# A block of 128 tokens in plain float32 products instead of split ones, with the steps around it in a new order

## The chip, the core and the metric

One NeuronCore of a Trainium2 chip runs the whole program. The metric is the device time of one execution in microseconds, lower is better. The engines are PE (TensorE, matmuls; PEld are its weight loads), DVE (VectorE), ACT (ScalarE), POOL (GpSimd) and SP (SyncE, which issues most DMAs).

## The reference

Three layers in a row on two sequences of 768 tokens (S) with 512 features (D):

```python
# 1. attention in 8 heads, each query only sees keys of its own cluster
scores = np.where(q_assign[..., :, None] == k_assign[..., None, :], scale * q @ k.T, -1e9)
x = softmax(scores) @ v
# 2. gate by a causal convolution over 5 tokens
gate = sigmoid(sum(conv_w[k] * shifted(x, k) for k in range(5)))
x = (gate * (x @ w_val)) @ w_out
# 3. one of 8 experts for each token; a token may keep the expert of the token before it
fresh = argmax(x[s] @ w_gate)
e = fresh if s == 0 or sigmoid(x[s] @ w_local) < 0.5 else prev
out[s] = softmax(x[s] @ w_gate)[e] * (relu(x[s] @ w1[e]) @ w2[e])
```

The choice of the expert hangs on small differences, so products that lead to it are made to float32 accuracy.

## The kernel before, in words

**Stages.** `Attn` (to about 286 us) goes through 8 pairs of heads. `Moe.rest` (286 to 396 us) finishes the last head pair and runs layer 2 for the second sequence, the router (`Route`) and the first block of tokens of layer 3. `Ffn.run` (from 396 us) takes the eight experts one after another, the one with the most tokens first.

**Splits.** A product to float32 accuracy is made of the engine's faster type F32R: each operand is split into a rounded part (`hi`, ACT copies it) and the remainder (`lo`, a subtraction). For the weights, `Ffn.split` (L1344) does this for a slice of 128 x 1024 numbers; eight slices make one expert: slices 0 to 3 are w1 (512 x 256 each), slices 4 to 7 are w2 (256 x 512 each).

**The block that goes ahead.** When the first sequence is routed, `Route.first` (L1089) picks 128 tokens of its most used expert. This is the block with r = -1. It is gathered (`gather`, tile xg-1), turned by PE (`turn`, tile pt-1, L1310), put through w1 (`up`, tiles ph-1, L1383 and L1386) and w2 (`down`, tile po-1, L1422) while the second sequence is still being routed. Its eight slices are ws0 to ws7; their remainders wl0 to wl7 are made on POOL in pieces of 256 columns, those of all later slices (from ws8) on DVE in one piece (L1352 to L1354). Slice buffers `ws` are eight in all (`Ffn.NS`): ws8 takes the place of ws0, and so on.

**The router.** For each half of a sequence (384 tokens, named 00, 01, 10, 11) the chain goes back and forth between PE and DVE: logits (lg, L872, PE), the code of each token's choice (L879 to L966, DVE), a row of codes (row, L972, PE), a running maximum over the tokens (cm, L977, DVE), back to columns (pb, L986, PE), one-hot choices (r_oh, L991 to L994, DVE), the count of equal choices ahead of a token (pp, L1008, PE), the position (r_pos, L1010 to L1014, DVE). `Route.placed` (L1045) makes from it the operands rhs and onr of a product (L1077: plf, plm and pll, PE) that writes the lists of tokens. After half 11, `Route.last` (L1136) ranks the experts into `tbl` (L1157), which SP reads before it can load any slice from ws8 on, and writes the lists `L`; then POOL gathers the tokens of expert 0 (xg0, L1296), PE turns them (pt0), and ACT and DVE write them as x0 (L1313, L1314). The first product with x0 and wh8 (L1378) begins the experts.

**What sets the order.** Each engine runs its instructions in the order in which the program issues them. In the attention that order comes from tables of places (`PLAN`, `LATE`, `MORE`, `FIRST`, `LAG`, `ORDER`, `GO`, and `BESIDE` for layer 2 of the first sequence); in `Moe.rest` from the table `STEPS`, a list of (name, count): each entry advances the named step so many times. `Y` is the product with w_out (tile yp, L858), `V` that with w_val (va, L825), `W` turns rows for the store to `ydr` (yr, L887), `conv` the convolution of the second sequence on DVE (L796), `split` one call of `Ffn.split`.

Of the kernel before, what the change touches and what calls it, by code (L numbers as in the profile page):

```python
# [20 lines left out]
DM = 512  # L21
# [26 lines left out]
class Attn:  # L48
# [1220 lines left out]
class Ffn:  # L1269
# [31 lines left out]
    def turn(self, ps, tag, pool, r, i, width=None):  # L1301

        nc, n = self.nc, self.cap(r)
        if i == 0:
            self.x[r] = pool.tile([128, KD, width or 2 * max(CAPS)], F32R, tag="x", name=f"x{r}")
        x, c0 = self.x[r], 128 * i
        m = min(128, n - c0)
        pt = ps.tile([128, 512], F32, tag=tag, name=f"pt{r}_{i}").rearrange("p (k t) -> p k t", k=KD)
        for k in range(KD):
            nc.tensor.transpose(pt[:, k, :m], self.xg[r][i][:m, 128 * k:128 * k + 128],  # L1310
                                self.rt.ident[:m, :m])
        hv = x[:, :, c0:c0 + m]
        nc.scalar.activation(hv, pt[:, :, :m], AF.Copy)  # L1313
        nc.vector.tensor_tensor(x[:, :, n + c0:n + c0 + m], pt[:, :, :m], f32(hv), op=ALU.subtract)  # L1314
# [29 lines left out]
    def split(self, pool, s, eng=None):  # L1344
# [10 lines left out]
        self.sp[s] = hi, lo  # L1355


    def up(self, ps, pool, r, c):
# [4 lines left out]
        if c == 0:  # L1363
            self.h[r] = [pool.tile([128, KF, 128 if r < 0 else max(CAPS)], F32R, tag=t, name=f"{t}{r}", bufs=1)
                         for t in ("hh", "hl")]
        hh, hl = (t[:, 2 * c:2 * c + 2, :n] for t in self.h[r])
        one = r < 0
        ps = ps.tile([128, 512 if one else 1024], F32, tag="h", name=f"ph{r}_{c}").rearrange(
            "p (m n) -> p m n", m=2)
        for m in range(2):  # L1370
# [3 lines left out]
            for k in range(KD):  # L1374
# [184 lines left out]
class Moe:  # L1559
# [75 lines left out]
    def rest(self, end, close, close_x):  # L1635
# [244 lines left out]
```

## Time and profile before

| | us |
|---|---|
| median of 3 runs | 582.47 |
| the three runs | 583.67, 578.79, 582.47 |
| the profiled execution, its own time | 579.11 |
| its span, first to last instruction | 577.3 |
| around the span | 1.81 |

All durations below are from the profiled execution. Its time lies 3.36 us under the median of the three. Times in rows are counted from the start of the span. An engine's row in a timeline gives the start, the duration, the line and operation, the tile written and the tiles read, how many neighbours are merged (x4), and in brackets how long the engine sat idle before and who released it.

### The profile page before, as it was taken

How to read it: one execution, taken by the hardware profiler on the slowest of the kernel's cores; microseconds unless marked ns; L12 is line 12 of the kernel's file. 1: busy time of each engine (PE TensorE's matmuls, PEld its weight loads, DVE VectorE, ACT ScalarE, POOL GpSimd, SP SyncE). 2: the span in 40 equal slices, each digit the busy share in tenths (PEclk: the TensorE clock that was granted, in tenths of full speed). 3: DMA queues.
4: the chain of work that ended last, by engine and by line, in shares of the span. 5: the costliest groups of instructions: out<-in, count | busy, mean ns of one | idle time of the engine just before them, and what ended most of it. 6: DMA issues, size and time to landing. Idle time of an engine off the chain costs nothing. (4 is left out here: it accounts for less than half of the span.)

```text
span 577.3 us, 9419 instructions
## 1 busy us (share of the span) xinstructions
PE 526.6 (91%) x3336; PEld 392.0 (68%) x3336; DVE 404.9 (70%) x703; ACT 303.2 (53%) x581; POOL 284.0 (49%) x227
## 2 busy tenths in 40 slices
PE   3798989999999999999988999699999999999993
PEld 0564545565555565567577898588989889879892
DVE  3756777888788779757967665886637486587681
ACT  2635454555545566576553244345635467468571
POOL 4475639795979698568920116735003043022011
PEclk9998899999999999899998999799999999999997
DMA  8996283857575625000000047058773877646940
GB/s 192 212 218 188 90 228 103 238 124 201 161 194 131 166 70 138 1 11 1 0 10 0 12 143 267 19 194 272 256 241 119 280 234 231 212 151 215 320 164 13
DMA packets 53180, 86.90 MB, mean 151 GB/s; under 512 B 6313, under 2 KB 30321, under 8 KB 53132
## 3 DMA queue, kind: packets, MB, share of 16 engines
q1 hardware_dynamic: 49996, 78.36, 46.8%
q0 software_dynamic: 3136, 7.92, 4.4%
q8 instruction: 27, 0.44, 0.3%
q14 instruction: 21, 0.17, 0.1%
HBM read 59.65 MB, written 8.62 MB: 118 GB/s over the span
## 5 line engine op out<-in xcount | busy, mean ns | idle before, releaser
L307 DVE TENSOR_REDUCE mn<-mx 128x1 f32<-128x512 f32 (+1 forms) x156 | 94.2, 638 | 31.9 <-PE mx L303 31.8
L398 ACT ACTIVATE p<-s 128x384 f32<-128x384 f32 x168 | 75.7, 486 | 59.5 <-PE s L397 57.6
L476 POOL TENSOR_TENSOR acc<-acc,p 128x768 f32<-128x768 f32 x42 | 85.4, 2054 | 4.2 <-ACT p L398 2.4
L1354 DVE TENSOR_TENSOR wl<-ws,wh 128x1024 fp32r<-128x1024 f32 x64 | 77.4, 1221 | 10.4 <-ACT wh L1349 9.3
L1349 ACT ACTIVATE wh<-ws 128x1024 fp32r<-128x1024 f32 x72 | 74.8, 1056 | 2.4 <-DMA ws<-in_w_dram 2.4
L396 PE MATMUL s<-xq,xk 128*128 128x384 f32 x168 | 64.0, 381 | 6.0 <-ACT p L398 6.0
L1455 POOL DMA_INDIRECT out_dram<-o,L x12 | 13.8, 1153 | 110.8 <-ACT o L1454 93.8
L492 PE MATMUL pv<-p,v 128*64 128x384 f32 x336 | 65.3, 511 | 0.0
L303 PE MATMUL mx<-km,q 80*128 80x512 f32 (+1 forms) x192 | 61.2, 388 | 3.1 <-DVE mn L307 2.8
L396 PEld LDWEIGHTS s<-xq,xk 128*128 128x128 f32 x168 | 31.8, 189 | 38.4 <-issue 22.0
L796 DVE SCALAR_TENSOR_TENSOR gp<-xT,cwt,gp 128x767 f32<-128x767 f32 (+3 forms) x32 | 52.8, 1665 | 6.7 <-ACT gp L790 6.3
L397 PE MATMUL s<-q,km 97*128 97x384 f32 x168 | 57.5, 342 | 0.0
L1383 PE MATMUL ph<-x,wh 128*128 128x384 f32 (+4 forms) x192 | 56.4, 338 | 0.0
L1386 PE MATMUL ph<-x,wl 128*128 128x256 f32 x192 | 51.6, 279 | 0.0
L303 PEld LDWEIGHTS mx<-km,q 80*128 80x128 f32 x192 | 37.4, 207 | 16.1 <-DVE mn L307 8.9
L1422 PE MATMUL po<-wh,hh 128*128 128x512 f32 x96 | 39.0, 406 | 0.0
L492 PEld LDWEIGHTS pv<-p,v 128*64 128x64 f32 x336 | 20.9, 140 | 26.5 <-issue 25.7
L1383 PEld LDWEIGHTS ph<-x,wh 128*128 128x128 f32 x192 | 36.1, 188 | 3.2 <-issue 1.0
L476 POOL TENSOR_TENSOR acc<-p,p 128x768 f32<-128x768 f32 x14 | 26.8, 1928 | 22.4 <-ACT p L398 22.4
L1422 PE MATMUL po<-wh,hl 128*128 128x512 f32 x96 | 37.8, 393 | 0.0
L1422 PE MATMUL po<-wl,hh 128*128 128x512 f32 x96 | 37.6, 391 | 0.0
L1386 PEld LDWEIGHTS ph<-x,wl 128*128 128x128 f32 x192 | 36.0, 188 | 0.1
(376 smaller groups left out, 1162.4 us busy)
## 6 DMA issues: line engine op xcount, KB each, us to landing
ws<-in_w_dram SPq DMA_DIRECT2D x72, 512.0 KB
qt<-in_qT_dram SPq DMA_DIRECT2D x8, 384.0 KB
kt<-in_kT_dram SPq DMA_DIRECT2D x8, 384.0 KB
q<-hiq SPq DMA_DIRECT2D x16, 192.0 KB
km<-hik SPq DMA_DIRECT2D x16, 192.0 KB
v<-in_v_dram SPq DMA_DIRECT2D x8, 384.0 KB
xk<-kt SPq DMA_DIRECT2D x16, 192.0 KB
xk<-hik SPq DMA_DIRECT2D x16, 192.0 KB
```

Source lines behind the costliest of these rows:

```text
L303: nc.tensor.matmul(ps[:, n * p:n * p + n], lhsT=q2[0:80, h, t * 128:t * 128 + 128], rhs=km[0:80, h, c:c + n], start=(p == 0), stop=True, s ...
L307: nc.vector.tensor_reduce(out=out, in_=src, axis=AX.X, op=ALU.max)
L396: nc.tensor.matmul(ps, lhsT=kl[:, h, ks], rhs=t1[:, h, hs], start=True, stop=False)
L397: nc.tensor.matmul(ps, lhsT=km[:97, h, ks], rhs=q2[:97, h, hs], start=False, stop=True)
L398: nc.scalar.activation(pt[:, h, hs], ps, AF.Exp, scale=1.0 / D ** 0.5)
L476: eng.tensor_tensor(t[:, h], p(0)[:, h] if first is None else t[:, h], p(j)[:, h], op=ALU.add)
L492: nc.tensor.matmul(self.pvt[64 * h:64 * h + 64, i, :HS], lhsT=v[:, j, 64 * h:64 * h + 64], rhs=pt[:, h, half(i)], start=False, stop=(j == ...
L1349: nc.scalar.activation(hi, t, AF.Copy)
L1354: (eng or nc.vector).tensor_tensor(lo[:, cs], t[:, cs], f32(hi[:, cs]), op=ALU.subtract)
L1383: nc.tensor.matmul(ps[:, m, :2 * n], lhsT=hi[:, k, ms], rhs=x[:, k, :2 * n], start=st and not (one and m), stop=False, skip_group_check=True)
L1386: nc.tensor.matmul(ps[:, m, :256], lhsT=lo[:, k, ms], rhs=x[:, k, :256], start=False, stop=sp, skip_group_check=True)
L1422: nc.tensor.matmul(self.po[r][i][:m], lhsT=a[:, k, ts], rhs=w[:, q], start=(k == 0 and z == 0), stop=(k == KF - 1 and z == 2))
```

## The change

The block r = -1 loses its splits. `Ffn.turn` makes x-1 as one float32 tile of 128 columns (no remainder on DVE). `Ffn.up_ahead` multiplies the slices ws0 to ws3 as they were loaded with x-1, 128 columns at a time, and one ACT Relu writes the hidden values. `Ffn.down_ahead` multiplies the hidden values with ws4 to ws7 in one pass. So the eight calls of `split` for ws0 to ws7 go: eight ACT copies (L1349) and 32 POOL subtractions (L1354), and with them four ACT copies and eight DVE operations on hidden values (L1391, L1392, L1402). The buffers ws0 to ws7 are now read by PE and free when it has read them. The experts' own path (`up`, `down`) stays as it is. The tables are written anew; a line of one of them stands in the diff.

```diff
-    LAG = (7, 10, 14, 12, 28, 6, 12, 12)
+    LAG = (7, 10, 14, 12, 28, 6, 13, 13)
...
-    def turn(self, ps, tag, pool, r, i, width=None):
+    def turn(self, ps, tag, pool, r, i):
...
-            self.x[r] = pool.tile([128, KD, width or 2 * max(CAPS)], F32R, tag="x", name=f"x{r}")
+            self.x[r] = pool.tile([128, KD, 2 * max(CAPS) if r >= 0 else n],
+                                  F32R if r >= 0 else F32, tag="x", name=f"x{r}")
...
         nc.scalar.activation(hv, pt[:, :, :m], AF.Copy)
+        if r < 0:
+            return
         nc.vector.tensor_tensor(x[:, :, n + c0:n + c0 + m], pt[:, :, :m], f32(hv), op=ALU.subtract)
...
-        n = 1024 if eng is None or eng is nc.vector else 256
-        for c in range(0, 1024, n):
-            cs = slice(c, c + n)
-            (eng or nc.vector).tensor_tensor(lo[:, cs], t[:, cs], f32(hi[:, cs]), op=ALU.subtract)
+        nc.vector.tensor_tensor(lo, t, f32(hi), op=ALU.subtract)
...
+    def up_ahead(self, ps, pool, c):
+        nc, x = self.nc, self.x[-1]
+        w = self.st[c].rearrange("p (k f) -> p k f", k=KD)
...
+        for m in range(2):
+            if m:
+                yield
+            for k in range(KD):
+                nc.tensor.matmul(ps[:, m], lhsT=w[:, k, 128 * m:128 * m + 128], rhs=x[:, k],
+                                 start=(k == m == 0), stop=(k == KD - 1), skip_group_check=True)
+        self.late[c] = lambda: nc.scalar.activation(self.h[-1][:, 2 * c:2 * c + 2], ps[:, 0:2],
+                                                    AF.Relu)
+
+    def down_ahead(self, ps, c):
+        nc = self.nc
+        w = self.st[4 + c].rearrange("p (k f) -> p k f", k=2)
...
+        for q in range(2):
+            k = 2 * c + q
+            nc.tensor.matmul(self.po[-1][0], lhsT=self.h[-1][:, k], rhs=w[:, q], start=(k == 0),
+                             stop=(k == KF - 1))
...
-        split = lambda i: self.f.split(self.wp, i, nc.gpsimd if i < 8 else nc.vector)
+        split = lambda i: self.f.split(self.wp, i)
...
-            "split": each(*((split, i) for i in range(11))),
+            "split": each(*((split, i) for i in range(8, 11))),
```

What the change moves, on three engines. First PE, from the logits of half 11 to the first products of the block, before (an F32R product of 256 columns each, four pairs of which make one half of a slice):

```order
L872 MATMUL lg11_3873<-yT11_3691,wg_416 32x96 x16
L1077 MATMUL plm_3903<-rhsm_3833,onrm_3826 128x48 x3
L1310 MATMUL pt-1_0_3909<-ident_63,xg-1_0_3655 128x128 x4
L887 MATMUL yr101_3922<-ident_63,yT10_3600 128x128 x4
L887 MATMUL yr102_3930<-ident_63,yT10_3600 128x128 x4
L972 MATMUL row11_3945<-ident_63,r_code_2954 1x4x32 x3
L1383 MATMUL ph-1_0_3953<-x-1_3908,wh0_3657 128x256
L1386 MATMUL ph-1_0_3953<-x-1_3908,wl0_3658 128x256
```

and now (lines are those of the changed kernel; L1368 is the product of `up_ahead`):

```order
L887 MATMUL yr101_3824<-ident_63,yT10_3536 128x128 x4
L872 MATMUL lg11_3832<-yT11_3670,wg_416 32x96 x16
L1312 MATMUL pt-1_0_3850<-ident_63,xg-1_0_3665 128x128 x4
L1077 MATMUL plm_3869<-rhsm_3801,onrm_3794 128x48 x3
L972 MATMUL row11_3874<-ident_63,r_code_2954 1x4x32 x3
L1368 MATMUL ph-1_0_3881<-x-1_3849,ws0_3596 128x128 x4
L887 MATMUL yr102_3892<-ident_63,yT10_3536 128x128 x4
L986 MATMUL pb11_3900<-rconst_2942,cm11_3878 32x1 x12
```

One of the row turns now stands ahead of lg11 and one behind row11, the turn of the block ahead of plm, and four float32 products of 128 columns stand where eight F32R products of 256 columns stood.

Second POOL, between the gather of the block and those of expert 0, before (the subtractions of ws0 to ws7):

```order
L1296 DMA xg-1_0_3655<-ydr_62,LA_2962 128x512
L1354 TENSOR_TENSOR wl0_3658<-ws0_3571,wh0_3657 128x256 x4
L1354 TENSOR_TENSOR wl1_3665<-ws1_3573,wh1_3664 128x256 x4
L1354 TENSOR_TENSOR wl2_3672<-ws2_3575,wh2_3671 128x256 x4
L1354 TENSOR_TENSOR wl3_3730<-ws3_3577,wh3_3729 128x256 x4
L1354 TENSOR_TENSOR wl4_3757<-ws4_3579,wh4_3756 128x256 x4
L1354 TENSOR_TENSOR wl5_3818<-ws5_3581,wh5_3817 128x256 x4
L1354 TENSOR_TENSOR wl6_3859<-ws6_3583,wh6_3858 128x256 x4
L1354 TENSOR_TENSOR wl7_3939<-ws7_3585,wh7_3938 128x256 x4
L1296 DMA xg0_0_4131<-ydr_62,L_2963 128x512
```

and now:

```order
L1296 DMA xg-1_0_3665<-ydr_62,LA_2962 128x512
L1296 DMA xg0_0_4042<-ydr_62,L_2963 128x512
L1296 DMA xg0_1_4044<-ydr_62,L_2963 128x512
L1296 DMA xg0_2_4046<-ydr_62,L_2963 64x512
L1296 DMA xg1_0_4135<-ydr_62,L_2963 128x512
```

POOL has no arithmetic left between the gathers.

Third DVE, at the end of the stage, from the remainder of ws8 on (x0 are the tokens of expert 0, LR lists for the stores, L1323 a copy in `tbl` that SP reads ahead of the load of ws11), before:

```order
L1354 TENSOR_TENSOR wl8_4152<-ws8_4071,wh8_4151 128x1024
L1402 SCALAR_TENSOR_TENSOR hl-1_3952<-hs-1_2_4128,hh-1_3951 128x256
L1392 TENSOR_TENSOR hs-1_3_4174<-ph-1_3_4157,hs-1_3_4174 128x2x128
L1402 SCALAR_TENSOR_TENSOR hl-1_3952<-hs-1_3_4174,hh-1_3951 128x256
L1184 TENSOR_SCALAR LR32_2964<-plr_4192,rconst_2942 128x24
L1186 COPY LR32_2964<-plr_4192 128x24
L1184 TENSOR_SCALAR LR64_2965<-plr_4192,rconst_2942 128x24
L1186 COPY LR64_2965<-plr_4192 128x24
L1314 TENSOR_TENSOR x0_4203<-pt0_0_4204,x0_4203 128x4x128
L1323 COPY tbl_2961<-tbl_2961 1x1
L1314 TENSOR_TENSOR x0_4203<-pt0_1_4237,x0_4203 128x4x128
L1314 TENSOR_TENSOR x0_4203<-pt0_2_4244,x0_4203 128x4x64
```

and now:

```order
L1354 TENSOR_TENSOR wl8_4062<-ws8_4036,wh8_4061 128x1024
L1327 COPY tbl_2961<-tbl_2961 1x1
L1318 TENSOR_TENSOR x0_4094<-pt0_0_4095,x0_4094 128x4x128
L1184 TENSOR_SCALAR LR32_2964<-plr_4102,rconst_2942 128x24
L1186 COPY LR32_2964<-plr_4102 128x24
L1184 TENSOR_SCALAR LR64_2965<-plr_4102,rconst_2942 128x24
L1186 COPY LR64_2965<-plr_4102 128x24
L1354 TENSOR_TENSOR wl9_4114<-ws9_4038,wh9_4113 128x1024
L1318 TENSOR_TENSOR x0_4094<-pt0_1_4117,x0_4094 128x4x128
L1318 TENSOR_TENSOR x0_4094<-pt0_2_4124,x0_4094 128x4x64
```

The copy in `tbl` comes directly behind wl8, the block's own operations are gone, and the remainder of ws9 now stands ahead of the last two thirds of x0; before, it came behind them.

## Rows read from the trace of the kernel before

**Rows 1.** The page, part 1: busy us, share of the span and instructions.

```profile
PE 526.6 (91%) x3336; PEld 392.0 (68%) x3336; DVE 404.9 (70%) x703; ACT 303.2 (53%) x581; POOL 284.0 (49%) x227
```

**Rows 2.** Windows by stage: stretch, length, busy us (count) of PE, PEld, DVE, ACT, POOL, PE clock, DMA, GB/s.

```profile
302.00:310.00 8.00, 4.44 (x24) 4.12 (x24) 5.12 (x5) 3.61 (x7) 1.83 (x1) 1.00 0.00 0
...
320.00:353.00 33.00, 33.00 (x289) 30.59 (x290) 18.89 (x72) 12.60 (x22) 5.28 (x4) 1.00 0.39 137
...
366.00:376.00 10.00, 5.62 (x27) 4.73 (x28) 7.38 (x18) 2.48 (x6) 6.18 (x9) 0.66 0.08 31
...
397.00:562.00 165.00, 165.00 (x1118) 143.39 (x1117) 111.67 (x153) 101.03 (x165) 33.17 (x27) 1.00 0.69 226
```

**Rows 3.** Timeline of PE, 353 to 397 us.

```profile
357.55 0.82 PE L972 MATMUL row<-ident,r_code 128*1 128x128 f32 x6 [1.42 <-DVE r_code L966]
...
361.62 0.35 PE L1008 MATMUL pp<-r_oh,r_tri 128*128 128x24 bf16 x8 [0.45 <-DVE r_oh L994]
...
364.58 0.87 PE L872 MATMUL lg<-yT,wg 128*32 128x96 f32 x32
...
370.38 1.49 PE L1077 MATMUL plm<-rhsm,onrm 128*128 128x48 f32 x6 [4.94 <-DVE rhsm L1068]
...
378.70 0.35 PE L1008 MATMUL pp<-r_oh,r_tri 128*128 128x24 bf16 x8 [1.02 <-DVE r_oh L994]
...
391.93 0.66 PE L1310 MATMUL pt<-ident,xg 128*128 128x128 f32 x4 [0.90 <-DMA xg<-ydr,L]
392.34 0.48 PE L1422 MATMUL po-1_0_4179<-wh,hh-1_3951 128*128 128x512 f32 x1
...
396.22 0.35 PE L1378 MATMUL ph<-x,wh 128*128 128x320 f32 x1
```

**Rows 4.** Timeline of POOL, the subtractions of ws0 to ws6.

```profile
352.50 19.69 POOL L1354 TENSOR_TENSOR wl<-ws,wh 128x256 fp32r<-128x256 f32 x28 [0.59 <-ACT wh L1349]
```

**Rows 5.** Windows around single steps of the router on DVE, columns as in rows 2.

```profile
314.95:316.50 1.55, 1.55 (x10) 1.55 (x11) 1.36 (x8) 1.23 (x2) 0.00 (x0) 1.00 0.00 0
353.88:357.41 3.53, 2.25 (x12) 1.92 (x12) 3.35 (x9) 0.81 (x2) 3.53 (x7) 1.00 0.93 345
335.91:336.60 0.69, 0.69 (x6) 0.69 (x5) 0.62 (x7) 0.69 (x1) 0.00 (x0) 1.00 0.00 0
364.93:370.24 5.31, 0.52 (x27) 0.30 (x16) 5.14 (x9) 1.24 (x2) 5.31 (x9) 0.83 0.13 49
380.25:382.04 1.79, 1.79 (x18) 1.79 (x17) 1.55 (x9) 1.42 (x3) 0.00 (x0) 1.00 0.05 9
382.04:383.89 1.85, 1.77 (x15) 1.56 (x14) 1.68 (x9) 0.38 (x1) 0.00 (x0) 1.00 0.75 278
385.03:386.13 1.10, 1.10 (x12) 1.10 (x11) 0.98 (x7) 0.21 (x1) 0.00 (x0) 1.00 0.75 225
```

**Rows 6.** Windows around runs of products on PE, columns as in rows 2.

```profile
348.26:349.62 1.36, 1.36 (x13) 1.36 (x13) 0.00 (x0) 0.00 (x0) 0.00 (x0) 1.00 0.98 323
385.71:387.60 1.89, 1.89 (x18) 1.89 (x17) 1.64 (x7) 0.69 (x2) 1.04 (x2) 1.00 1.04 356
387.60:390.40 2.81, 2.81 (x14) 2.09 (x12) 2.74 (x8) 1.64 (x3) 2.50 (x2) 1.00 0.99 348
422.93:426.53 3.60, 3.60 (x33) 2.21 (x32) 0.77 (x1) 0.00 (x0) 0.00 (x0) 1.00 0.62 193
552.44:554.33 1.89, 1.89 (x65) 1.69 (x64) 1.89 (x3) 0.91 (x1) 0.00 (x0) 1.00 0.77 281
```

**Rows 7.** Timelines of SP, ACT and DVE, 383 to 399 us.

```profile
383.90 11.35 SPq L1334 DMA_DIRECT2D ws<-in_w_dram  x4
...
387.60 1.06 ACT L1349 ACTIVATE wh<-ws 128x1024 fp32r<-128x1024 f32 x1 [0.99 <-DMA ws<-in_w_dram]
...
395.08 1.02 DVE L1314 TENSOR_TENSOR x<-pt,x 128x512 fp32r<-128x512 f32 x2 [1.09 <-ACT x L1313]
396.30 2.36 DVE L1354 TENSOR_TENSOR wl<-ws,wh 128x1024 fp32r<-128x1024 f32 x2 [0.20 <-ACT wh L1349]
```

More of the change, by code (lines that the diff above doesn't have):

```diff
@@ L1342, in load, with split @@
         self.st[s] = t
-    def split(self, pool, s, eng=None):
+    def split(self, pool, s):
         nc = self.nc
@@ L1363, in up @@
         if c == 0:
-            self.h[r] = [pool.tile([128, KF, 128 if r < 0 else max(CAPS)], F32R, tag=t, name=f"{t}{r}", bufs=1)
+            self.h[r] = [pool.tile([128, KF, max(CAPS)], F32R, tag=t, name=f"{t}{r}", bufs=1)
                          for t in ("hh", "hl")]
         hh, hl = (t[:, 2 * c:2 * c + 2, :n] for t in self.h[r])
-        one = r < 0
-        ps = ps.tile([128, 512 if one else 1024], F32, tag="h", name=f"ph{r}_{c}").rearrange(
+        ps = ps.tile([128, 1024], F32, tag="h", name=f"ph{r}_{c}").rearrange(
             "p (m n) -> p m n", m=2)
@@ L1383, in up @@
                     nc.tensor.matmul(ps[:, m, :2 * n], lhsT=hi[:, k, ms], rhs=x[:, k, :2 * n],
-                                     start=st and not (one and m), stop=False,
+                                     start=st, stop=False,
                                      skip_group_check=True)
@@ L1630, in conv @@
         return self.m.conv(self.gates, self.x[1][m], 1, m)
-    STEPS = (("S02", 1), ("end", 7), ("S03", 1), ("G02", 1), ("V03", 3), ("end", 2), ("V03", 1), ("x", 2), ("G03", 1), ("psum", 1), ("S10", 1), ("V10", 4), ("G10", 1), ("conv", 3), ("Y00", 4), ("conv", 2), ("Y00", 4), ("conv", 2), ("Y00", 4), ("conv", 2), ("Y00", 4), ("conv", 2), ("Y01", 4), ("L00", 1), ("R00", 1), ("conv", 2), ("Y01", 4), ("R00", 1), ("conv", 2), ("Y01", 4), ("R00", 1), ("conv", 2), ("Y01", 4), ("R00", 1), ("conv", 9), ("V11", 2), ("L01", 1), ("R01", 1), ("V11", 2), ("G11", 1), ("R01", 1), ("W00", 2), ("V12", 2), ("R01", 1), ("V12", 2), ("G12", 1), ("E00", 1), ("E01", 1), ("R01", 1), ("W00", 1), ("W01", 1), ("first", 1), ("V13", 3), ("W01", 1), ("V13", 1), ("W01", 1), ("G13", 1), ("E00", 1), ("E01", 1), ("first", 1), ("weights", 1), ("Y10", 8), ("Y10", 4), ("Y10", 2), ("first", 1), ("Y10", 2), ("gather", 1), ("split", 3), ("Y11", 4), ("L10", 1), ("R10", 1), ("E10", 1), ("split", 1), ("Y11", 4), ("R10", 1), ("split", 1), ("Y11", 2), ("R10", 1), ("Y11", 2), ("E10", 1), ("R10", 1), ("split", 1), ("more", 1), ("Y11", 4), ("ahead", 1), ("split", 1), ("W10", 1), ("L11", 1), ("R11", 1), ("more", 1), ("turn-1", 1), ("E11", 1), ("W10", 2), ("split", 1), ("R11", 1), ("up0", 1), ("R11", 1), ("E11", 1), ("W11", 1), ("R11", 1), ("last", 2), ("up0", 1), ("W11", 2), ("loads", 1), ("up1", 2), ("up0", 1), ("up2", 1), ("last", 1), ("up2", 1), ("gather", 1), ("up1", 1), ("last", 1), ("gather", 1), ("split", 1), ("up2", 1), ("up3", 3), ("down", 2), ("last", 1), ("turn", 1), ("loads", 1), ("down", 1), ("turn", 2), ("down", 1), ("split", 2), ("store", 1))
@@ L1692, in up @@
         def up(c):
-            yield from self.f.up(pa["ps"], pa["sb"], -1, c)
+            yield from self.f.up_ahead(pa["ps"], pa["sb"], c)
             yield
@@ L1730, in rest @@
             "gather": each(*((lambda r=r: self.f.gather(self.pg, r),) for r in range(-1, 2))),
-            "split": each(*((split, i) for i in range(11))),
-            "turn-1": each((lambda: self.f.turn(pa["ps"], "h", pa["sb"], -1, 0, 256),)),
+            "split": each(*((split, i) for i in range(8, 11))),
+            "turn-1": each((lambda: self.f.turn(pa["ps"], "h", pa["sb"], -1, 0),)),
             "turn": each(*((turn, i) for i in range(3))),
             "loads": each((loads, 8, 11), (again,)),
-            "down": each(*((lambda c=c: self.f.down(pa["ps"], -1, c),) for c in range(4))),
+            "down": each(*((lambda c=c: self.f.down_ahead(pa["ps"], c),) for c in range(4))),
             "store": each((lambda: self.f.store(pa["sb"], -1),)),
```

20 lines of the change are left out of this document (13 added, 7 removed).

## The prediction, on record before the changed kernel ran

> **What bounds the kernel now.** I read four views in this order. The page's first part comes first [rows 1]: PE is busy 526.6 of 577.3 us, so nearly every microsecond that the kernel can lose or win is one in which PE waits or runs slowly. The second view is the windows by stage [rows 2]. From 397 to 562 us, the experts, PE is busy 165.00 of 165.00: whatever moves the start of the experts moves the end by as much. From 320 to 353 us it is busy 33.00 of 33.00, so a new order there can win nothing by itself. From 302 to 310 us it is busy 4.44 of 8.00, and from 366 to 376 us 5.62 of 10.00, with a mean granted clock of 0.66. The third view is PE's timeline between 353 and 397 us [rows 3]. Its brackets name what PE waited for: 1.42 us for r_code, 0.45 and 1.02 for r_oh, 4.94 for rhsm, all written by DVE in the router's chain, and 0.90 for the gathered tokens of expert 0. Together 8.73 us. The fourth view says why DVE is late. POOL makes the remainders wl0 to wl6 in 28 pieces from 352.50 on, 19.69 us, or 0.70 us a piece [rows 4]. Beside them the same DVE steps take far longer than where POOL is idle [rows 5]: the code of half 10 takes 3.53 us (353.88 to 357.41), that of half 00 1.55; `placed` for half 10 takes 5.31 us (364.93 to 370.24), for half 11 1.85. These are steps of seven to nine small operations. So POOL's subtractions, which nobody waits for at that moment, hold up DVE, and DVE holds up PE.
>
> **What the change removes.** All 32 pieces on POOL go. I take the free durations for every router step from 353 us on. Then the code of half 10 comes 2.0 us earlier, more than the 1.42 that PE waited for it; the 0.45 for r_oh goes likewise. So lg11, which ends at 365.45 [rows 3], ends at about 363.6. Behind it 4.94 + 1.02 + 0.90 = 6.86 us of waits are at stake. With them goes a stretch at the lower clock: after the 4.94 us wait, the six plm products take 1.49 us, while twelve of that shape took 1.36 at 348.26 [rows 3, 6]. The 5.62 busy us of the window up to 376 us were almost all spent at 1.2 GHz instead of 2.4 GHz [rows 2]; half of some 5 us is 2.5 us lost. In all 1.87 + 6.86 + 2.5 = 11.2 us can go. The eight ACT copies and the block's DVE operations go too; ACT and DVE are not the bound there, so I count them at nothing.
>
> **What the products cost.** Before, w1 takes 64 F32R products of 256 columns, 16 in 1.89 us, or 0.118 each, the load of its weights hidden behind it; w2 takes 24 of 512 columns, 12 in 2.81, or 0.234 each [rows 6]. That is 7.6 + 5.6 = 13.2 us. Now each float32 product runs as two (the trace has twelve plf where the program has six). w1 needs 32 x 2 = 64 of 128 columns, w2 8 x 2 = 16 of 512. No row has exactly this shape. Four with 32-column weights side by side, 128 columns, take 1.89/16 = 0.118 us; two with 64-column weights, 256 columns, take 3.60/16 = 0.225 [rows 6]. So 128 columns need 0.118 and 512 need 0.45, if the load is hidden. What the load takes is bounded by plf: 50 columns behind 128-column weights, 0.113 each. Lower end: 0.113 and 0.45. Upper end, load and product one after the other: 0.231 and 0.56. I take 0.118 and 0.45, because the row nearest in shape, F32R with 128 x 128 weights and a product of the same 0.118 us, hides its load. Sum: 64 x 0.118 + 16 x 0.45 = 14.8 us, 1.6 more than before. With the upper end it is 23.8 us, 10.6 more than before.
>
> A rule of the Trainium skill speaks against that choice. "TensorE: Matmul & The Clock Gate", section "The mechanism", says that a weight load overlaps matmuls in flight only when it goes to another group of rows; here all 128 rows are used each time. By the rule the sum would be at the upper end; the 16 F32R products in 1.89 us, each with a load of its own on all rows, speak for the lower one, and the page's part on LDWEIGHTS also knows a background buffer.
>
> **What is late next.** Three waits are left, from the new order. Four row turns on PE take 0.4 us (391.93 to 392.34 [rows 3]), and so I take 0.4 for the turn of the block too.
> First row11: once pp10 is done, DVE needs the position (0.69 [rows 5], 0.9 with a subtraction), `placed` 1.85 and the code of half 11 1.55, together 4.3 us; PE has in that time three yp products (0.5), two groups of row turns (0.8), lg11 (0.8), the turn of the block (0.4) and plm (0.7), 3.2 us. PE waits 1.1.
> Second pll: after pp11 DVE needs 0.9 + 1.79 (the ranks and `tbl`) + 1.85 = 4.5 us [rows 5]; PE has two groups of row turns and 24 products of the block, 0.8 + 2.8 = 3.6. PE waits 0.9.
> Third x0: the lists are ready 1.10 us behind pll [rows 5], and x0 was complete at 395.08 + 1.02 = 396.10, 10.0 us after them [rows 5, 7]. The remainder of ws9 now stands ahead of the last two thirds of x0: 1.2 us more (2.36 for two [rows 7]), 12.3 in all. PE has 24 products of w1 (2.8), w2 (7.2), three turns (1.2) and a small product of lists (0.5), 11.7. PE waits 0.6.
> Together 2.6 us. The weights are not late. ws8 is issued when `tbl` is read (383.90) and used at 387.60 [rows 7]; its buffer, ws0, is free when half 11 still waits for its choices. ws12 to ws15 need the products of w2 to be done, but their first use is a whole set of `up` products later.
>
> **The rest of the tables.** The order on SP does not change; on POOL a subtraction for k goes behind a sum once in each of five pairs, on ACT an exponential ahead of a rounding copy. From 296 to 310 us DVE's convolution steps stay in one chain with ACT's scaling ahead of them, so the wait there [rows 2] moves by some tenths. I count all this at 0; it could be 2 us either way.
>
> **The sum.** -11.2 + 1.6 + 2.6 = -7.0 us. Laying the steps of the new order one behind the other with the same durations, I come to -7.2 to -8.8 at the start of the experts, since some of the waits overlap; I forecast -7.5. From the profiled execution's 579.11 that is 571.6. That execution was one of the quicker: the median of the runs shown is 3.36 higher, which gives 575.0. I predict the middle, 573.3 us; on the same footing no change would be 573.3 + 7.5 = 580.8, and the rivals are counted from there. A measurement of this kernel can tell about 1% (5.8 us) from no change, so faster means under 576.6 and slower over 588.3.
>
> **The rivals.**
> A: the weight load is not hidden. 80 x 0.113 = 9.0 us more on PE, of which the waits for pll and x0 absorb 0.9 + 0.6 = 1.5: -7.5 + 7.5 = 0, 580.8. For it: no row has a float32 product on all 128 rows that is longer than its load. Against it: the F32R products, which load as often and hide it. Chance 0.14. It is the Trainium skill's rule above.
> B: DVE is not slowed by POOL but by something else at that time, such as the transfers (345 GB/s in the window at 353.88 [rows 5]). Then the code and `placed` stay long, and only 1.6 us of dearer products is added: 582.4. Against it: the window at 382.04 has 278 GB/s and is quick, and that at 364.93 has 49 and is slow. Chance 0.04.
> C: the tables give back what the router wins, each of five pairs 1 us: -7.5 + 5 = -2.5, 578.3. For it: only that they are touched; against it: SP's order is the same. Chance 0.11.
> D, the slower side: the clock. The place is PE from row11 on. It waits there for 1.1 us and twice more within 20 us; if the grant falls at the first wait and stays low until the experts begin, some 20 us of work take 40, which hides the 1.5 us of the two later waits: -7.5 + 20 - 1.5 = +11.0, 591.8. It decides from 7.5 us of work at the lower level on, where the gain is eaten. For it: the grant fell after the wait of 4.94 [rows 2, 3]. Against it: it came back within 6 us of work, and 1.1 is a quarter of that wait. Chance 0.09.
>
> **How the numbers follow.** The forecast has 0.62, all of it over 1% faster. A, B and C end within 1%: 0.14 + 0.04 + 0.11 = 0.29. D is slower: 0.09. The low end takes the full 11.2 with no new wait and the quick run: 579.1 - 11.2 = 567.9, and 1 for the tables, 567. The high end reaches through C and A: 581.
>
> **What would show it.** On DVE, `placed` for half 10 takes about 1.9 us and the code 1.6. PE's wait for rhsm is under 1 us, and its clock from 353 us on is 1.00. The w1 products of the block stand 0.118 apart, those of w2 0.45. The first product of expert 0 starts near 388.7 instead of 396.22, and from there PE is busy without a gap. I am wrong if the first expert starts where it did, if the products stand 0.2 apart, or if the stage up to 353 us has moved by over 2 us.

## The result, and the profile after

The changed kernel takes 563.71 us (median of 4 runs, 560.5 to 565.96), the kernel before on the same chip 582.87 (578.79 to 583.67): a ratio of 0.9734 with a 95% interval of 0.9688 to 0.978, or 15.5 us less (12.8 to 18.2). The two medians alone would give 0.9671 and 19.2 us, which lies outside that interval; the record does not say which runs the ratio was formed from. I go by the ratio: against the kernel before in the later experiments (medians 579.08 and 579.34 us, seven runs each) 563.71 us is 0.973, and the two profiled executions are 15.2 us apart. Forecast were 573.3 us and 7.5 us less, with a range from 567 to 581 us. The profiled execution took 563.89 us, its span 562.1.

The profile after, first the page's part 1 (busy us, share of the span, instructions), to set beside [rows 1]:

```profile
PE 522.1 (93%) x3328; PEld 387.0 (69%) x3328; DVE 387.3 (69%) x694; ACT 293.8 (52%) x569; POOL 257.9 (46%) x195
```

Then the windows by stage, columns as in [rows 2]: the stretch around the first products with w_out, the stage up to the logits of half 10, the router with the block, the experts.

```profile
296.00:304.00 8.00, 6.43 (x37) 6.11 (x37) 6.13 (x7) 3.66 (x7) 1.88 (x1) 1.00 0.00 0
...
314.00:347.00 33.00, 32.57 (x287) 30.23 (x287) 17.68 (x75) 11.13 (x20) 4.76 (x3) 1.00 0.45 158
347.00:381.00 34.00, 31.08 (x286) 23.89 (x286) 19.96 (x87) 12.80 (x24) 6.39 (x7) 1.00 0.55 192
381.10:546.00 164.90, 164.90 (x1116) 143.29 (x1115) 110.15 (x150) 98.79 (x163) 32.57 (x27) 1.00 0.66 220
```

PE is still the bound (522.1 of 562.1), the experts have no gap, and the granted clock stays at 1.00 through the router. PE's timeline from the logits of half 10 to the first expert, answering to [rows 3]:

```profile
345.04 0.87 PE L872 MATMUL lg<-yT,wg 128*32 128x96 f32 x32
...
356.70 0.77 PE L1077 MATMUL plm<-rhsm,onrm 128*128 128x48 f32 x6
358.05 0.82 PE L972 MATMUL row<-ident,r_code 128*1 128x128 f32 x6 [0.58 <-DVE r_lacc L1086]
...
366.76 0.84 PE L1077 MATMUL pll<-rhsl,onrl 128*128 128x48 f32 x6 [0.73 <-DVE rhsl L1068]
...
368.39 1.95 PE L1368 MATMUL ph-1_3_4052<-x-1_3849,ws 128*128 128x128 f32 x16
370.18 5.32 PE L1380 MATMUL po-1_4067<-ws,hh-1_3880 128*128 128x512 f32 x12
...
380.75 0.42 PE L1403 MATMUL ph<-x,wh 128*128 128x320 f32 x1 [1.46 <-DVE x L1318]
```

The wait of 4.94 us for rhsm is gone; three waits of 0.58, 0.73 and 1.46 us are left. Windows around single steps: the code of half 11, `placed` for half 10 (columns DVE third, POOL fifth), then sixteen products of w1 and twelve of w2:

```profile
356.35:357.88 1.53, 1.12 (x10) 0.99 (x9) 1.36 (x9) 0.60 (x1) 0.00 (x0) 1.00 0.84 315
354.49:356.34 1.85, 1.71 (x39) 1.20 (x38) 1.68 (x8) 1.47 (x3) 0.00 (x0) 1.00 0.05 21
...
368.39:370.18 1.79, 1.79 (x18) 1.79 (x17) 1.72 (x8) 0.00 (x0) 0.88 (x1) 1.00 1.04 357
370.18:375.33 5.15, 5.15 (x14) 2.23 (x13) 1.43 (x5) 1.60 (x3) 3.93 (x5) 1.00 0.83 287
```

`placed` takes 1.85 us instead of 5.31 [rows 5], the product of w1 1.79 / 16 = 0.112 us, that of w2 5.15 / 12 = 0.43.

**Where the time went.** I cut every trace at instructions that all kernels have, by their starts in PE's timeline: the turn mt (L321) of the sixth and of the seventh pair of heads, the first logits (half 00), the logits of half 10, the first product of expert 0. From there to PE's end it is 171.3 us before and 171.4 after. All lengths in us, of one profiled execution each; the experiments stand in the same table:

| kernel | to mt 6 | mt 6 to mt 7 | to first logits | to logits 10 | to expert 0 | ratio to before |
|---|---|---|---|---|---|---|
| before | 214.21 | 28.34 | 71.47 | 38.94 | 43.26 | 1 |
| after | 213.54 | 25.25 | 67.31 | 38.94 | 35.71 | 0.9734 |
| e1 attention as before | 219.40 | 28.32 | 66.78 | 38.94 | 35.76 | 0.987 |
| e6 the same again | 218.41 | 26.75 | 66.78 | 38.97 | 36.04 | 0.9772 |
| e2 steps as before | 216.27 | 25.23 | 69.92 | 38.96 | 35.72 | 0.9779 |
| e3 block and tail alone | 212.74 | 26.76 | 71.48 | 38.95 | 35.62 | 0.9855 |
| e4 before, no subtractions | 222.01 | 26.71 | 69.92 | 38.91 | 32.71 | 0.9809 |
| e5 POOL's work back | 217.08 | 25.26 | 65.55 | 38.97 | 41.26 | 0.9826 |
| e7 tail reordered | 217.45 | 25.24 | 65.56 | 38.94 | 35.11 | 0.9697 |
| e8 all reordered | 216.69 | 25.25 | 65.85 | 40.38 | 34.33 | 0.9706 |
| e9 x0 as before | 215.64 | 26.91 | 67.27 | 38.97 | 35.80 | one run |
| e10 PLAN as before | 215.13 | 25.46 | 66.77 | 38.95 | 35.67 | one run |
| e11 before, x0 moved | 215.24 | 25.53 | 71.47 | 38.97 | 44.94 | one run |
| e12 convolution ahead | 217.27 | 25.25 | 70.55 | 38.93 | 35.68 | one run |

Before against after: 0.67 + 3.09 + 4.16 + 0 + 7.55 = 15.47 us. The last column but one is what I had forecast, 7.5 us. The other half was won ahead of the logits of half 10, where I had counted nothing. Each trace is one execution, and the columns move between executions: the kernel before and e11 run the same instructions in the last column and take 43.26 and 44.94 us. What is chance in a column is said with the experiments.

### The profile page after: what moved, and what is told of

It is laid out like the page before. It is cut to its first block, busy times and chain, and to the rows that moved or that the text cites. A ratio compares the mean times of both kernels' runs of the same rounds, so it can differ in the third digit from the quotient of the medians.

```text
span 562.1 us, 9334 instructions
## 1 busy us (share of the span) xinstructions
PE 522.1 (93%) x3328; PEld 387.0 (69%) x3328; DVE 387.3 (69%) x694; ACT 293.8 (52%) x569; POOL 257.9 (46%) x195
## 3 DMA queue, kind: packets, MB, share of 16 engines
q0 software_dynamic: 3136, 7.92, 4.4%
## 5 line engine op out<-in xcount | busy, mean ns | idle before, releaser
L1354 DVE TENSOR_TENSOR wl<-ws,wh 128x1024 fp32r<-128x1024 f32 x64 | 77.5, 1222 | 11.0 <-ACT wh L1353 9.8
L1353 ACT ACTIVATE wh<-ws 128x1024 fp32r<-128x1024 f32 x64 | 66.6, 1056 | 6.3 <-DMA ws<-in_w_dram 6.3
L1480 POOL DMA_INDIRECT out_dram<-o,L x12 | 14.5, 1212 | 112.5 <-ACT o L1479 99.2
L396 PEld LDWEIGHTS s<-xq,xk 128*128 128x128 f32 x168 | 32.0, 191 | 34.7 <-issue 19.2
L796 DVE SCALAR_TENSOR_TENSOR gp<-xT,cwt,gp 128x767 f32<-128x767 f32 (+3 forms) x32 | 51.5, 1625 | 2.5 <-ACT gp L790 2.1
```

What stands on the lines that cost most here:

```text
L396: nc.tensor.matmul(ps, lhsT=kl[:, h, ks], rhs=t1[:, h, hs], start=True, stop=False)
L1354: nc.vector.tensor_tensor(lo, t, f32(hi), op=ALU.subtract)
```

## The experiments

By the tail I mean the last column, from the logits of half 10 to expert 0. The theory after the result: **T**, the tail's 7.55 us come from POOL's subtractions, less what the new block costs; the rest comes from the tables. Rivals: the rest is chance of one execution (R); the tail's gain is in the lighter work of the other engines (P).

**e1 and e6: the changed kernel with the attention's tables of before,** the same kernel twice.

```diff
-    LAG = (7, 10, 14, 12, 28, 6, 13, 13)
+    LAG = (7, 10, 14, 12, 28, 6, 12, 12)
...
```

(PLAN, LATE, MORE, FIRST, ORDER, GO and BESIDE likewise.)

> The changed kernel, with the eight tables of the attention as they were before. In the traces the last product rb of the attention (L556) came at 291.68 us before and at 287.52 now. Theory T (the attention's tables give 4 us): rb at about 291.7, the time 4.2 us above that of the changed kernel, ratio to before about 0.981. Rival R (the 4 us are the chance of one profiled execution, 1.1 of them the arrival of the first transfers): rb at 287 to 288.5, ratio 0.973.

> The same kernel as e1_attention_as_before once more. There the turn mt of the sixth pair came at 219.40 us, with the same instructions up to it at 212.74 in e3_block_and_tail_alone. Theory C (chance: the arrival of the first transfers, the moment at which PE gets fast, stretches at the lower clock): mt at another place, between 212 and 222, and the time moves with it; from that turn on the way is the same as in the first run to 1.6 us: 28.3 or 26.7 to the next mt, 49.9 to the last rb, 16.8 to the first logits. Theory T (this program's own tables or addresses make it slow): mt near 219.4 and 571 us again, ratio 0.987.

e1 took 571.2 us, ratio 0.987 (0.9815 to 0.9924), e6 566.48, ratio 0.9772 (0.9747 to 0.9796): the intervals of one and the same kernel do not overlap. Up to the first mt of the table the five traces with the old tables lie between 212.74 and 222.01 us, with the same instructions in each. So chance decides there (C), and an interval from the runs of one loading of the program is too narrow. Whether it goes by the loading, by the chip (e1 and e6 ran on two) or by the single execution is not shown: e1's four runs lie within 3 us, e4's between 565.04 and 572.64. The 0.67 us of that column say nothing. The two profiled executions are 2.2 us apart: in e6 mt 6 came 1.0 us earlier than in e1, the next column is 1.6 us shorter and the tail 0.3 longer. That next column repeats better: 26.7 or 28.3 us with the old tables, 25.2 to 25.3 with the new.

**e2: the old order of steps up to the gather of the block.** The entries of STEPS up to ("gather", 1) are those of before, then ("Y11", 4), ("L10", 1) and the new ones.

> The changed kernel, with the order of steps up to the gather of the block as it was before (attention's tables and everything behind the gather stay new). In the traces the way from rb to the first logits took 22.3 us before (291.68 to 314.02) and 18.6 now. Theory T (the place of the convolution's steps among the products of w_out decides how long PE waits for yT): the waits of 1.65 and 2.37 us come back, 3.8 us more, ratio to before about 0.980. Rival R (those waits depend on what the attention leaves behind, not on this order): one wait of some 1.6 us, ratio 0.973.

Ratio 0.9779 (0.9725 to 0.9833). Both waits came back (1.66 and 2.37 us), and mt 7 to the first logits took 69.92 us instead of 65.55 to 67.31. T holds. The size needs like beside like, since PE's clock falls behind the second wait in most traces with the old order: the granted clock is 0.57 from 310.20 to 314.20 us in the kernel before, and 0.57 at the same place in e2 and e3. In e4 below, with the same old order, it stays at 1.00, and the column has 69.92 us where before and e3 have 71.5. e4 against e1 and e6 (66.78), all three with the old attention and a clock of 1.00, leaves 3.1 us to the order of steps; e3 against e1 (4.7) has the fall of the clock in it.

**e3: block and tail alone,** e1's and e2's edits together.

> Only the float32 block, the loss of its splits and the order behind the logits of half 10 are new; all tables up to there are those of before. Theory T (what was forecast, 7.5 us, comes from here alone, and the rest from the tables): first logits at about 314.0, expert 0 at 388.7, ratio to before 0.987. Rival R (the tables up to there give nothing): ratio 0.973. Rival S (the tail's gain needs the earlier tables): ratio 0.995 or more.

Ratio 0.9855 (0.9802 to 0.9909), expected 0.987 by T; the tail took 35.62 us as in the changed kernel, the column ahead of the first logits 71.48 us as in the kernel before. R and S fall: what was forecast is there by itself, and without the new tables there is no more.

**e4: the kernel before without its subtractions.**

```diff
...
+            if eng is nc.gpsimd:
+                continue
             (eng or nc.vector).tensor_tensor(lo[:, cs], t[:, cs], f32(hi[:, cs]), op=ALU.subtract)
-        self.sp[s] = hi, lo
+        self.sp[s] = (hi, hi) if eng is nc.gpsimd else (hi, lo)
```

> The kernel before without the 32 subtractions on POOL: the remainders wl0 to wl7 are not computed, and the products that read them read wh0 to wh7 in their place; the number of products is the same. Theory T (POOL's work slows the small DVE operations of the router): placed for half 10 falls from 5.31 to about 1.9 us, PE's wait of 4.94 us for rhsm to under 1, expert 0 starts 7 to 9 us earlier, ratio to before about 0.986. Rival B (something else slows DVE, such as the transfers): placed stays near 5 us, ratio 1.000. Rival P (the product count is what matters): ratio 1.000.

Ratio 0.9809 (0.9734 to 0.9884). The tail fell from 43.26 to 32.71 us with the old order and the old products. PE's timeline of e4, same place as [rows 3]:

```profile
357.55 0.87 PE L872 MATMUL lg<-yT,wg 128*32 128x96 f32 x32
...
367.86 0.87 PE L1077 MATMUL plm<-rhsm,onrm 128*128 128x48 f32 x6
...
385.96 0.66 PE L1310 MATMUL pt<-ident,xg 128*128 128x128 f32 x4 [1.21 <-DMA xg<-ydr,L]
...
390.26 0.35 PE L1380 MATMUL ph<-x,wh 128*128 128x320 f32 x1
```

plm has no bracket: of the router's four waits none is left, only one of 1.21 us for the gather. `placed` for half 10 takes 1.85 us (365.35 to 367.20) instead of 5.31. B and P fall: every product and every transfer was still there. POOL's subtractions cost 10.55 us in this pair of traces.

**e5: POOL's work put back into the changed kernel.**

```diff
...
+            for c in range(0, 1024, 256):
+                nc.gpsimd.tensor_tensor(pa["busy"], t[:, c:c + 256], t[:, c:c + 256],
+                                        op=ALU.subtract)
...
```

(The rest of the edit puts this for each of ws0 to ws7 at the old places of the splits in STEPS.)

> The changed kernel with POOL's work put back: 32 subtractions of 128 x 256 from ws0 to ws7 into a scratch tile that nobody reads, at the places in the order of steps that the splits had. From the logits of half 10 to the first product of expert 0 the changed kernel takes 35.71 us, the kernel before 43.26, the kernel before without its subtractions 32.71. Theory T (POOL's work beside DVE's small operations costs about 10 us): 43 to 46 us, ratio to before 0.986 to 0.992, placed for half 10 over 3.5 us instead of 1.85. Rival P (the gain comes from the lighter work of DVE and ACT, not from POOL): 36 to 37 us, ratio 0.973 to 0.976.

Ratio 0.9826 (0.9783 to 0.9868); the tail took 41.26 us, 5.55 more, less than the 43 to 46 expected but far from P's 36 to 37. `placed` for half 10 took 3.26 us, also a little less than the 3.5 expected. POOL's timeline, the window of `placed` (columns as above), and DVE's code of half 11:

```profile
347.41 22.42 POOL L1742 TENSOR_TENSOR busy<-ws 128x256 fp32r<-128x256 f32 x32
```

```profile
357.74:361.00 3.26, 1.75 (x40) 1.21 (x38) 3.09 (x9) 1.45 (x3) 2.87 (x6) 1.00 0.43 161
```

```profile
361.44 0.18 DVE L960 TENSOR_TENSOR t_eq<-lgt,t_mx 128x24 f32<-128x24 f32 x1
361.66 0.60 DVE L961 TENSOR_TENSOR t_eq<-t_eq,rconst 128x24 f32<-128x24 f32 x1
362.29 0.18 DVE L962 TENSOR_REDUCE t_m<-t_eq 128x3 f32<-128x24 f32 x1
362.38 0.54 DVE L963 TENSOR_TENSOR t_nk<-lgt,rconst 128x3 f32<-128x3 f32 x1
362.85 0.15 DVE L964 TENSOR_TENSOR t_m<-t_m,rconst 128x3 f32<-128x3 f32 x1
363.03 0.58 DVE L966 TENSOR_TENSOR r_code<-t_m,t_nk 128x3 f32<-128x3 f32 x1
```

Without POOL the same steps of the changed kernel:

```profile
357.10 0.18 DVE L961 TENSOR_TENSOR t_eq<-t_eq,rconst 128x24 f32<-128x24 f32 x1
...
357.41 0.15 DVE L963 TENSOR_TENSOR t_nk<-lgt,rconst 128x3 f32<-128x3 f32 x1
...
357.72 0.16 DVE L966 TENSOR_TENSOR r_code<-t_m,t_nk 128x3 f32<-128x3 f32 x1
```

Three of the five operations with two inputs take 0.54 to 0.60 us instead of 0.15 to 0.18, and each of the three ends 0.02 to 0.04 us after the POOL piece beside it (pieces from 361.60 to 362.22, 362.29 to 362.91 and 362.98 to 363.60 us). The other two and the reduction are not held up.

This also shows why less came back than e4 took away. In e5 a piece takes 0.61 us and the next begins 0.08 us after its end, and some of DVE's operations slip through; POOL is busy 2.87 of the 3.26 us. In the kernel before a piece takes 0.72 us or more, the next begins ahead of its end (POOL busy 5.31 of 5.31 [rows 5]), and all seven operations of `placed` are held up. So PE waited 1.65 us for rhsm in e5, not 4.94. The pieces of e5 read one tile twice, those of before two tiles; whether that makes the difference is not shown.

**e7 and e8: can the three new waits be filled?** In e7 four products go ahead of row11, four each ahead of pb11 and pll, and the turns of expert 0 ahead of the remainder of ws9; e8 adds two edits ahead of the first logits.

```diff
-("more", 1), ("R11", 1), ("up0", 1), ("E11", 1), ("W10", 1), ("R11", 1), ("up0", 1)
+("more", 1), ("up0", 1), ("R11", 1), ("E11", 1), ("W10", 1), ("up0", 1), ("R11", 1)
...
-("turn", 1), ("last", 1), ("split", 1), ("turn", 2), ("split", 1)
+("turn", 2), ("last", 1), ("turn", 1), ("split", 2)
```

> The changed kernel with three pieces of the order behind the logits of half 11 moved: products of the block into the waits for row11 and pll, and the turns of expert 0 and its x0 ahead of the remainder of ws9. Theory W (the waits of 0.58, 0.73 and 1.46 us are what the new order costs, and other work can fill them): from the logits of half 10 to expert 0 33.2 to 33.8 us instead of 35.71, ratio to before about 0.970. Rival L (the chain through DVE, POOL and the gather sets the start of expert 0): the waits move, 35.2 to 35.7 us, ratio 0.973.

> As e7_tail_reordered, and two more pieces: the end of the attention's last pair goes ahead of the second sigmoid and the gate of chunk 2 again, and the sigmoid of the convolution behind the third output of w_out. Theory W: the wait for rt falls from 1.71 to about 0.7 us, the wait for yT of 1.57 goes, expert 0 starts another 2.0 to 2.6 us earlier than in e7 counted from the turn mt of the seventh pair, ratio to before about 0.966. Rival L: the waits reappear at row00 or at later yT copies, and the gain over e7 is under 1 us.

e7: ratio 0.9697 (0.967 to 0.9724), e8 0.9706 (0.9668 to 0.9745). The three waits went, and a wait for the gather took their place. PE's timeline of e7:

```profile
378.32 0.63 PE L1312 MATMUL pt<-ident,xg 128*128 128x128 f32 x4 [1.45 <-DMA xg<-ydr,L]
```

The tail became 35.11 and 34.33 us, 0.6 and 1.4 less. e7 lies at L's 35.2, not at W's 33.2 to 33.8, so L holds. Both have the lowest ratios measured, but against 0.9734 the difference lies within the intervals; it isn't shown in time. e8's other two edits gave nothing, and L holds there too (139.61 us from mt 7 to expert 0 in e7, 140.56 in e8): the wait for rt fell from 1.71 to 0.66, and three waits of 0.36 to 0.81 appeared (yT, row00, the logits of half 01), so that the column to logits 10 grew by 1.4.

**e9, e10 and e11: which table gives the 1.5 to 3 us between mt 6 and mt 7?** In e11 the edit of the kernel before is this one entry; in e9 the changed kernel has it back:

```diff
...
-("x0", ((6, 2),))
+("x0", ((6, 11),))
...
```

> The changed kernel with one entry of BESIDE as before: the split x0 (an ACT copy and a POOL subtraction q, L811) at place (6, 2) instead of (6, 11). Between the turns mt of the sixth and the seventh pair, all five traces with the new tables so far have 25.23 to 25.26 us, the five with the old ones 26.71 to 28.34. In the trace of before the POOL subtraction stood at 224.17 us beside a DVE step of the convolution (2.23 us instead of 1.01), and the sum behind it beside the next (2.29 instead of 0.98); now it stands at 227.58, behind both. Theory X (that entry alone makes the difference): 26.7 us, or 28.3 with a stretch at the lower clock. Rival Y (it is PLAN or another table): 25.25 us.

> The changed kernel with PLAN, LATE, MORE, LAG, FIRST, ORDER and GO as before; BESIDE stays new. Theory X: 25.25 us between the two turns. Rival Y: 26.7 to 28.3. On the time of the whole: within chance of the changed kernel, ratio 0.970 to 0.985 in a single run.

> The kernel before with nothing changed but the split x0 in BESIDE, at (6, 11) instead of (6, 2). Theory X: 25.2 us between the two turns instead of 26.7 to 28.3, no wait of 0.78 us for mn at the start of pair 7, all else as before (71.5 us from there to the first logits, 43.3 in the tail). Rival Y: 26.7 to 28.3.

26.91, 25.46 and 25.53 us (one trace each): X holds, one entry decides, in both kernels. PE's wait in the kernel before, then DVE and POOL there, two steps of the convolution (L796) and the subtraction q with the sums behind it:

```profile
230.17 0.50 PE L303 MATMUL mx<-km,q 80*128 80x256 f32 x2 [0.78 <-DVE mn L307]
```

```profile
224.58 2.23 DVE L796 SCALAR_TENSOR_TENSOR gp<-xT,cwt,gp 128x764 f32<-128x764 f32 x1
...
227.23 2.29 DVE L796 SCALAR_TENSOR_TENSOR gp<-xT,cwt,gp 128x767 f32<-128x767 f32 x1
```

```profile
224.17 1.82 POOL L811 TENSOR_TENSOR q<-xT,q 128x768 fp32r<-128x768 f32 x1
226.89 4.30 POOL L476 TENSOR_TENSOR acc<-p,p 128x768 f32<-128x768 f32 x2 [0.90 <-ACT p L398]
```

And of e11:

```profile
225.62 1.01 DVE L796 SCALAR_TENSOR_TENSOR gp<-xT,cwt,gp 128x764 f32<-128x764 f32 x1
...
227.04 0.98 DVE L796 SCALAR_TENSOR_TENSOR gp<-xT,cwt,gp 128x767 f32<-128x767 f32 x1
```

```profile
229.39 1.84 POOL L811 TENSOR_TENSOR q<-xT,q 128x768 fp32r<-128x768 f32 x1 [4.15 <-ACT q L810]
```

It is the same collision as in the router. In the kernel before, the maxima that PE waits for stood behind these two steps (0.78 us at 230.17), and in two of the six traces with the old place (before and e1) PE's clock fell as well (0.69 and 0.71 granted in the five us behind the wait, 1.00 in e3, e4, e6 and e9), which makes 28.3 of 26.7. The tail of e11 (44.94 instead of the 43.3 expected) has its old waits back, and a wait of 1.62 us for the gather, behind which the granted clock falls to 0.55 (390.30 to 394.00).

e10 shows one thing more, in the next column: with the old tables of the attention other than BESIDE it has 66.77 us, as e1 and e6 have 66.78, where e5 and e7 have 65.55 and 65.56. In all seven traces with these old tables PE waits in the seventh pair for probabilities p that ACT writes, in none of the seven with the new; here in the kernel before:

```profile
255.57 0.44 PE L396 MATMUL s<-xq,xk 128*128 128x384 f32 x1 [1.19 <-ACT p L398]
```

**e12: only the start of the convolution moved, in e2.**

```diff
...
-("V10", 4), ("G10", 1), ("conv", 3), ("Y00", 4)
+("V10", 4), ("conv", 3), ("G10", 1), ("Y00", 4)
...
```

> As e2_steps_as_before (the changed kernel with the old order of steps up to the gather), with one entry moved: the first three steps of the convolution stand ahead of the gate of chunk 0 of the second sequence instead of behind it. From the turn mt of the seventh pair to the first logits e2 took 69.92 us, the order of now 65.55 to 67.31. Theory V (the chain of the convolution begins too late, so the sigmoids hold up the copies yT on ACT): the waits of 1.66 and 2.37 us go, 65.5 to 67 us. Rival Z (the whole order is needed): over 69 us.

70.55 us: V falls. Instead of two waits there is one, as long, and the clock falls behind it; the copies yT now stand behind the gate's copy gh, which waits for DVE. PE's timeline and the window behind the wait:

```profile
303.85 0.69 PE L858 MATMUL yp<-xq,hw_out 128*128 128x384 f32 x1 [3.64 <-ACT yT L862]
```

```profile
304.00:308.00 4.00, 4.00 (x13) 4.00 (x14) 2.21 (x2) 1.85 (x3) 1.33 (x1) 0.50 0.00 0
```

Which entries of the new order make the 3.1 us is left open; this one alone does not.

## Why the prediction was right, and where it was wrong

**What bounds the kernel:** right. The stage of the experts is as long as before, and every microsecond at its start is one at the end.

**What the change removes,** forecast 11.2 us: e4 measured 10.55. The three parts of it, the waits for r_code and rhsm, the later ones and the stretch at the lower clock, all went with POOL's work alone. Rival B (transfers) is refuted, since e4 has them all.

**What the products cost,** forecast 14.8 us for both: the 64 of w1 stand 0.112 to 0.124 us apart, some 7.4 us, those of w2 take 5.15 us for twelve and 1.98 for the last four, 7.1: 14.5. Rival A would have had 0.23 and 0.56. The rule of the Trainium skill that stood behind it ("TensorE: Matmul & The Clock Gate", section "The mechanism") doesn't agree with the trace here: the loads on all 128 rows stay hidden, busy for 1.79 us beside the 1.79 us of sixteen products.

**What is late next,** forecast 1.1 + 0.9 + 0.6 = 2.6 us: 0.58 + 0.73 + 1.46 = 2.77, at the three places named. The single sizes were off by 0.5, 0.2 and 0.9 us, and that the sum fits is luck. Without POOL's work and with the old products the tail is e4's 32.71 us, and the new block costs 3.0 us more than that: 1.3 in products and, since e4 has a wait of 1.21 us itself, 1.6 in waits. So the plain float32 products are no gain in themselves: they are the price of getting POOL's work off DVE's way.

**The sum from the logits of half 10 on,** forecast -7.5: -7.55. The agreement to 0.05 us is luck. The new tail took 35.62 to 36.04 us in the eight traces that have it, the old one 43.26 and 44.94: 7.2 to 9.3 us.

**The rest of the tables: the step that failed.** I wrote that the wait at 302 to 310 us "moves by some tenths" and counted all tables "at 0; it could be 2 us either way". By the table they give 4.16 us from mt 7 to the first logits and 3.09 between the two mt. By one of the signs that I had named the forecast was wrong there: the stage up to the logits of half 10 moved by 7.92 us (352.96 to 345.04), not by less than 2.

From mt 7 to the first logits I had seen the wait [rows 2] and that it hangs on ACT, but not followed the new order of that one queue. PE waits twice for the copies yT in the kernel before, once after; first PE before and after, then ACT before and after:

```profile
303.37 0.45 PE L858 MATMUL yp<-xq,hw_out 128*128 128x384 f32 x1 [1.65 <-ACT yT L862]
...
310.18 0.49 PE L858 MATMUL yp<-xq,hw_out 128*128 128x384 f32 x1 [2.37 <-ACT yT L862]
```

```profile
303.29 0.45 PE L858 MATMUL yp<-xq,hw_out 128*128 128x384 f32 x1 [1.57 <-ACT yT L862]
```

```profile
308.08 0.84 ACT L803 ACTIVATE gp<-gp 128x768 f32<-128x768 f32 x1 [4.39 <-DVE gp L796]
...
309.66 0.85 ACT L862 ACTIVATE yT<-yp 128x384 f32<-128x384 f32 x2
```

```profile
301.19 0.84 ACT L803 ACTIVATE gp<-gp 128x768 f32<-128x768 f32 x1 [2.48 <-DVE gp L796]
...
302.76 0.85 ACT L862 ACTIVATE yT<-yp 128x384 f32<-128x384 f32 x2
305.68 0.49 ACT L862 ACTIVATE yT<-yp 128x384 f32<-128x384 f32 x1 [2.06 <-PE yp L858]
307.16 0.85 ACT L803 ACTIVATE gp<-gp 128x768 f32<-128x768 f32 x1 [0.98 <-DVE gp L796]
```

Before, the first copies stood behind the gate's copy gh (301.27) and a scaling, the next behind a sigmoid (308.08) that waited 4.39 us for DVE's convolution. Now the first stand ahead or right behind (295.51, 298.24), only the sigmoid at 301.19 still holds copies up, and the next one stands behind its copy. That the order of steps brings the waits back is shown by e2; this account of how is a reading of the two queues, and e12 did not confirm its nearest form.

Taken like beside like, the 4.16 us are 3.1 from the order of steps (e4 against e1 and e6), 1.2 from the attention's tables (e10 against e5 and e7), 1.5 because the clock did not fall (before against e4), less 1.7 for the wait of 1.57 us, which e5 and e7 do not have. Of the 3.09 us between the two mt 1.2 to 1.7 come from the entry x0 and 1.6 from a fall of the clock. So some 3 us of the gain are stretches at the lower clock which other executions with the same order did not have.

In the column between the two mt I had the mechanism in hand, POOL's work stretching DVE's, and looked for it in the router alone. Rival C (the tables give back 5 us) had the wrong sign; rival D (the clock falls at row11) didn't happen, the granted clock being 1.00 from 347 to 381 us. The forecast's side was right, its size half. The median measured, 563.71 us, lies 3.3 us under the low end of the range; the ratio, taken of the median shown ahead of the forecast (0.9734 x 582.47), comes out just at it, 567.0. That end stood for the full 11.2 us without a new wait and a quick run, so that the time reached it by the tables is luck.

## What to carry to other kernels

Where DVE runs a chain of small operations that PE waits for, look at what POOL does at that time: 22 us of POOL work that nobody waited for cost 10.55 us here, and moving one POOL subtraction by some 4 us gave 1.2 to 1.7, or 2.8 where the clock had fallen as well. When a change rewrites tables, follow the queue of each engine that stands at the end of a known wait, before counting the tables at nothing. Cut the traces at instructions that all kernels share: the sections repeat to some tenths, or move by 1.5 to 1.8 us for a reason that the trace names (a fall of the clock, a collision), where the whole moves by several us.

## What the runs showed of the hardware that was not expected

The collision of DVE and POOL goes either way. The same two instructions, at the same place of the same order, in the changed kernel and in e7, DVE first:

```profile
297.32 3.78 DVE L796 SCALAR_TENSOR_TENSOR gp<-xT,cwt,gp 128x765 f32<-128x765 f32 x2
```

```profile
298.41 1.88 POOL L845 TENSOR_TENSOR gl<-gp,gh 128x768 fp32r<-128x768 f32 x1 [9.43 <-ACT gh L844]
```

```profile
301.19 2.06 DVE L796 SCALAR_TENSOR_TENSOR gp<-xT,cwt,gp 128x765 f32<-128x765 f32 x2
```

```profile
302.28 2.69 POOL L845 TENSOR_TENSOR gl<-gp,gh 128x768 fp32r<-128x768 f32 x1 [9.44 <-ACT gh L844]
```

In the first DVE is held up by 1.7 us, and PE waits 1.57 us for yT; in the second POOL is, by 0.8, and PE doesn't wait. In both DVE's second step starts 0.05 us ahead of POOL's subtraction (298.36 and 298.41, 302.23 and 302.28), so the trace does not show what decides.

The Trainium skill, "SBUF — State Buffer", section "SBUF: two separate sides", has a rule for it: a DVE operation in a 2-port mode (one that uses both of DVE's pairs of ports), or with two inputs in SBUF while POOL reads SBUF, and a POOL operation need the same pair of ports, and the one that starts first holds it as an exclusive lock for the whole instruction. The held-up operations agree (each ends 0.02 to 0.04 us after POOL's piece in e5), and so does the reduction, 0.18 us with and without POOL. That the first to start wins is not borne out by the starts in the trace of the changed kernel.

The granted clock does not show everything. In e1 it reads 1.00 from 31.27 to 36.00 us, while products of 384 columns stand 0.32 us apart, as they do in e12 behind its wait at a granted 0.50; in the changed kernel the like stand 0.17 to 0.18 apart from 33.54 on. Part of the chance in the first column is when PE gets fast there: the same product starts at 35.19 us in e1 and 33.54 in the changed kernel, a later turn (L343) at 42.05 and 38.92, so that 1.5 of e1's 5.9 us arise between them. The rest is open.

```profile
31.91 0.52 PE L413 MATMUL s<-xq,xk 128*128 128x384 f32 x1
32.23 0.52 PE L423 MATMUL s<-q,km 97*128 97x384 f32 x1
```

```profile
31.27:36.00 4.73, 4.73 (x16) 3.94 (x15) 3.04 (x7) 2.35 (x6) 3.84 (x6) 1.00 1.04 251
```
